# Casting two pairs' queries earlier in the head of a fused retention and MLP kernel

## The chip, the cores and the metric

The kernel runs on one core of one Trainium2 chip. The metric is the device time of one execution in microseconds. The core has a matmul engine (PE, with its weight loads, PEld), a vector engine (DVE), an activation engine (ACT), a general engine (POOL) and a queue engine (SP), each with its own stream of instructions; they wait for each other by semaphores. DMA queues are fed by SP, ACT and POOL.

## The reference

The reference takes queries, keys and values for 8 batches, 8 heads, 576 positions and 64 channels, computes retention (causal scores weighted by a decay per head, with no softmax), and sends the result through a two-layer MLP with a hard-swish:

```python
scores = scale * np.matmul(q, k.transpose(0, 1, 3, 2))
gamma = 1.0 - 2.0 ** (-5.0 - np.arange(H, dtype=np.float32))
Dmat = np.where(rel >= 0, gamma[:, None, None] ** rel[None, :, :], 0.0)   # rel = i - j
ret = scores * Dmat[None, :, :, :]
attn = np.matmul(ret, v)
...
h = x @ w_in                      # 4608 x 512 times 512 x 2048
g = h * np.clip(h + 3.0, 0.0, 6.0) / 6.0
out = g @ w_out                   # 2048 x 512
```

All inputs and the output are float32.

## The kernel before

The 4608 tokens are cut into nine blocks of 512. Block 0, the "heads", holds the first 64 positions of all eight sequences. Blocks 1 to 8 hold positions 64 to 575 of one sequence each, in four chunks of 128. For each block the retention result is brought into a transposed tile `xT`; then come the up product with W_in ("up units", 16 per block, PE into `ph`, ACT makes `u`, DVE makes `g`) and the down product with W_out (`pd`, or in later blocks a Strassen scheme, `pm`).

The order of work on PE, DVE, POOL, ACT and SP is the order in which the program is written (`manual_schedule`); the semaphores are set by a dependency tracker. So a call that stands earlier in the text puts its instructions earlier on each engine that it uses, and an instruction that waits holds up all that follow on its engine.

The change is in the head, lines 738 to 766, where block 0 is prepared. Heads are treated in pairs, 0 to 3. For each pair:

- `load_half` (L403) issues the loads. The queries and pair 0's keys arrive as float32 by the SP and ACT queues, the other keys and the values as float16 by the POOL queue. SP issues one half of the queries of pairs 0 and 1 (ACT the other half) and both halves of pairs 2 and 3, in this order.
- `cast_heads` (L423) turns float32 into float16 on DVE: one instruction for pair 0's keys and one for each pair's queries (tile `hq`).
- `turn_heads` (L428) transposes with eight PE products against the permutation `by_chunk` (tiles `hptk`, `hptq`, in a PSUM pool of two buffers, so the third turn waits for the first's copy) and one copy on ACT or DVE to `hkT` or `hqT`.
- `mask_of_heads` (L123) makes two tiles of decay weights with two exponentials on ACT. Their tile is called `ws` in the profile, since it borrows that tile's memory.
- `scores_heads` (L459) is eight PE products into two PSUM banks (`hpa`) and two DVE products with the masks (L470, tile `ha`).
- `values_heads` (L451) permutes the values by 16 PE products (`hpv`) and copies them on ACT.
- `inner_heads` (L473) is eight PE products (`hpo`) and a copy to `xT`, on ACT or, for pair 2, on DVE.

`idle_products(n)` (L388) issues n pairs of 512-column products of the identity, the two of a pair in two halves of the array, whose result no one reads. Each call takes one buffer from the pool `pp` of six PSUM buffers, which the scores, values and inner products share in rotation.

Behind the head come the first four up units, interleaved over the four pairs' parts of `xT`, with pair 3's inner products in their middle; then units 4 to 15. W_in comes in four pieces of 512 KB on POOL's queue (the first in two halves), then W_out in four. A unit needs the piece of its number divided by four. The loads of chunks 4 to 7 wait on SP until the third issued piece of W_out has landed. While the down product of block 0 runs, POOL scales the queries and values of chunk 4 onward (L207, L210), ACT casts their keys (L203), and PE turns them (`ptk`, `ptq`).

Of the kernel before, what the change touches and what calls it, by code (L numbers as in the profile page):

```python
# [21 lines left out]
def kernel(  # L22
# [100 lines left out]
    def mask_of_heads(i):  # L123

        for h in (2 * i, 2 * i + 1):
            nc.scalar.activation(hmask[:, h, :], dist, ACTF.Exp, bias=scale, scale=float(np.log(gamma[h])))
# [37 lines left out]
    def product(out, lhs, rhs, **flags):  # L164

        for h2 in range(2):
            r = slice(h2 * D, h2 * D + D)
            nc.tensor.matmul(out[r], lhs[:, r], rhs, skip_group_check=True, **flags)  # L168
# [6 lines left out]
    def half_tile(pool, tag, i, dtype, name, **more):  # L175

        if (tag, i // 2) not in pair:
            pair[tag, i // 2] = pool.tile([P, 2, H * D], dtype, tag=tag, name=f"{name}{i // 2}", **more)
        return pair[tag, i // 2][:, i % 2]
# [208 lines left out]
    def idle_products(n):  # L388
        idle = psum.tile([P, NP, P], FP32, tag="pp", name="idle")
        for _ in range(n):  # L390
            product(idle, ident16, ident16.unsqueeze(1).to_broadcast([P, NP, P]), start=True, stop=True)
# [26 lines left out]
    def heads16(i, nm):  # L418
        if nm == "q":
            return half_tile(work, "q16", i, FP16, "hq16_", bufs=2).rearrange("p (e j d) -> p e j d", e=2, j=NJ)  # L420
        return work.tile([P, 2, NJ, D], FP16, tag=f"{nm}16", bufs=dict(k=4, v=NV16)[nm], name=f"h{nm}16_{i}")

    def cast_heads(i, nm, copy):  # L423
        t = heads16(i, nm)
        copy(t, hd[i][nm])  # L425
        hd[i][nm] = t

    def turn_heads(i, nm, copy):  # L428
        pt = psum.tile([P, NJ, P], FP32, tag="st", bufs=2, name=f"hpt{nm}{i}")
        for j in range(NJ):  # L430
            for e in range(2):
                nc.tensor.matmul(pt[e * D:e * D + D, j, :], hd[i][nm][:, e, j, :], by_chunk, start=True, stop=True,  # L432
                                 skip_group_check=True)
        x, y = (NCB, 2 * RP) if nm == "k" else (2 * NCB, RP)
        t = half_tile(work, "qT", i, FP16, "hqT", bufs=3) if nm == "q" else work.tile(
            [P, H * D], FP16, tag="kT", bufs=4, name=f"hkT{i}")
        t = t.rearrange("p (x j y) -> p x j y", x=x, j=NJ)
        copy(t, pt.rearrange("p j (x y) -> p x j y", y=y))  # L438
        hd[i][nm + "T"] = t
# [19 lines left out]
    def scores_heads(i):  # L459
        kT, qT = hd[i]["kT"], hd[i]["qT"]  # L460
        a16 = work.tile([P, 2, NCB, P], FP16, tag="a16", bufs=4, name=f"ha16_{i}")
        pa = [psum.tile([P, NCB, P], FP32, tag="pp", name=f"hpa{h2}_{i}") for h2 in range(2)]
        for c in range(NCB):
            for h2 in range(2):
                r = slice(h2 * D, h2 * D + D)
                nc.tensor.matmul(pa[h2][:, c, :], kT[r, c].rearrange("d j x -> d (j x)"),
                                 qT[r, 2 * c:2 * c + 2].rearrange("d e j r -> d (e j r)"), start=True, stop=True)
        for h2 in range(2):
            m = hmask[:, 2 * i + h2:2 * i + h2 + 1, :].to_broadcast([P, NCB, P])
            nc.vector.tensor_tensor(a16[:, h2], pa[h2], m, ALU.mult)  # L470
        hd[i]["a16"] = a16
# [249 lines left out]
    with tc.manual_schedule(engines={ENG.PE, ENG.DVE, ENG.Pool, ENG.Activation, ENG.SP}):  # L721
        sp, act, pool = nc.sync, nc.scalar, nc.gpsimd
        on_act, on_dve = nc.scalar.copy, nc.vector.tensor_copy
        indices()
        for nm in ("k", "q"):
            landed = load_half(0, nm, 0, sp)
            keys = landed if nm == "k" else keys
            load_half(0, nm, 1, act)
        nc.scalar.activation(warm, half, ACTF.Exp)
        load_half(1, "q", 0, sp)  # L730
        load_half(1, "q", 1, act)
        for i in (2, 3):
            for e in range(2):
                load_half(i, "q", e, sp, keys)
        for i, nm in ((1, "k"), (2, "k"), (3, "k"), (0, "v"), (1, "v"), (2, "v"), (3, "v")):
            for e in range(2):
                load_half(i, nm, e, pool, None if (i, nm) == (1, "k") else keys)
        win_piece(0, 2)
        distances()
        idle_products(5)  # L740
        mask_of_heads(0)
        cast_heads(0, "k", on_dve)
        turn_heads(0, "k", on_act)
        mask_of_heads(1)
        idle_products(3)
        cast_heads(0, "q", on_dve)
        turn_heads(0, "q", on_dve)
        turn_heads(1, "k", on_act)
        mask_of_heads(2)
        idle_products(1)  # L750
        cast_heads(1, "q", on_dve)
        turn_heads(1, "q", on_act)
        mask_of_heads(3)
        scores_heads(0)
        cast_heads(2, "q", on_dve)
        turn_heads(2, "k", on_act)
        scores_heads(1)
        turn_heads(2, "q", on_act)
        turn_heads(3, "k", on_act)
        cast_heads(3, "q", on_dve)  # L760
        scores_heads(2)
        turn_heads(3, "q", on_act)
        values_heads(0)
        scores_heads(3)
        values_heads(1)
        inner_heads(0, on_act)
        values_heads(2)
        inner_heads(1, on_act)
        win_piece(1)
        values_heads(3)  # L770
        inner_heads(2, on_dve)
        first = [up_steps(0, u) for u in range(4)]
        for dmc in range(3):
            for unit in first:
                next(unit)
            if dmc == 1:
                inner_heads(3, on_act)
        for unit in first:
            for _ in unit:
                pass  # L780
        for n in (2, 3):
            win_piece(n)
        wout = [wout_piece(pc) for pc in (0, 2, 1, 3)]
        decays()
        mask_of_chunk()
        others()
        fetch(8, wout[2])
        for u in range(4, NFC):
            up_unit(0, u)
        weight_sums(3)  # L790
        weight_sums(1, 2, 4)
        down = down_plain(0)
        go("k0 D4 k1 D4 +1 k2 D4 +1 k3 D6 h0 D2 c4 h1 D3 h2 D3 h3 D3 D4 c5 t4 D5 a4 s4 u4 D5 z4 t5 c6 D4 "
           "x4 a5 s5 i4 u5 z5 D5 t6 x5 D2 i5 D4 L2 c7 a6 s6 u6 L3 z6 D1 t7 L3 x6 a7 s7 i6 u7 D1 L1 z7 L2 c8 L1 D2 x7 D1 i7 t8 D3 "
           "R3 c9 R3 a8 s8 u8 R2 t9 z8 R4 c10 x8 a9 s9 i8 u9 U1 z9 c11 t10 U3",
           1, down)
        down = down_plain(1)
        go("c12 D6 x9 a10 s10 i9 u10 z10 D2 t11 c13 +1 D7 x10 a11 s11 i10 u11 z11 c14 +2 D8 x11 D2 i11 t12 +1 D3 +1 D3 "
           "a12 s12 u12 t13 D2 c15 D2 z12 +1 D4 x12 a13 s13 i12 u13 z13 D1",
           down=down)  # L800
        go("U1 D3 t14 U1 D2 U1 U1 D2 x13 a14 s14 i13 u14 z14 o1 c16 U1 D2 U1 D2 t15 U1 D2 U1 D2 +1 U1 x14 a15 s15 i14 u15 z15 "
           "c17 D2 U1 D2 +1 U1 D2 +1 U1 D2 x15 +1 U1 i15 t16 c18 +1 U1 D2 t17 U1 U1",
           2, down)
        for kb in range(2, NB):
            for _ in down:
                pass
            plain = kb < FIRST
            down = down_plain(kb) if plain else down_strassen(kb)
            per = 4 if plain else 7
            table = FIRST_STEADY if kb == 2 else STEADY  # L810
            c = NCB * (kb + 2)
            owed = 0
            for u in range(NFC):
                if u == 0:
                    owed += per - 2
                    for _ in range(per - 2):
                        next(down, None)
                if kb + 1 < NB:
                    up_unit(kb + 1, u)
                else:  # L820
                    side_sums(1)
                owed -= per
                while owed < 0:
                    next(down, None)
                    owed += 1
                for w, i in table.get(u, []):
                    if w == "D":
                        for _ in range(i):
                            next(down, None)
                        owed += i  # L830
                    else:
                        do([(w, i if w == "+" else c + i)])
        for _ in down:
            pass
# [30 lines left out]
```

## Time and profile before

The times of three runs are 301.63, 301.76 and 302.48 us, median 301.76. The profiled execution took 302.47 us; its span from the first to the last instruction is 300.7 us.

| What | Value |
|---|---|
| Median of three runs | 301.76 us |
| Profiled execution, its span | 302.47 us, 300.7 us |
| Mean granted PE clock | 0.989 |
| First up product | 18.51 us |
| First product of the keys for block 0's state (`hpk`), behind the last up unit | 33.92 us |
| Last idle time of PE by issue alone | 1.7 us, at 154.25 |

The page of the profile gives for each engine its busy time, its share of the span and its number of instructions, and then the chain that ended last, by engine. A table by stretches gives the busy time of each engine in each stretch, the granted clock (1.00 is full speed), the mean busy share of the DMA engines and their rate. A line of the time order gives the start, the time from the first start to the last end, the engine, the line, the operation, the tiles, the shapes and the count; in brackets is the idle time of the engine ahead of it and what ended it. A line of a DMA issue gives the tile, the queue, the count, the size, and the time from issue to landing.

### The profile page before, as it was taken

Reading aid. Unit: us, or ns where it says so; the run is one execution under the profiler, and the core shown is the slowest. Engines: PE = TensorE matmul, PEld = TensorE weight load, DVE = VectorE, ACT = ScalarE, POOL = GpSimd, SP = SyncE. Lnnn points to the kernel's source line nnn. Section 1 sums busy time; section 2 is a strip of 40 time slices with the busy share of each in tenths; the row PEclk is TensorE's granted clock in tenths of the full one; section 3 lists DMA queues with packets and bytes.
Section 4 is the critical chain, followed back from the end, with each engine's and each line's share of the span. In section 5 each row is a group of like instructions: output and inputs, shape, how many; then the busy total and the mean of one; then the engine's idle time right before and its main releaser. Section 6 shows DMA issues by size and latency. Waiting matters only on the chain.

```text
span 300.7 us, 12600 instructions
## 1 busy us (share of the span) xinstructions
PE 288.2 (96%) x5538; PEld 219.6 (73%) x5538; DVE 213.2 (71%) x387; ACT 196.2 (65%) x361; POOL 135.5 (45%) x176
## 2 busy tenths in 40 slices
PE   5799999899999999999979999999999999999995
PEld 2457666787556667877858878789788977778894
DVE  4728736769895688788875797678768776647554
ACT  4648875899866687586757577657765674565420
POOL 7975068517751912539621962375238003100510
PEclk9969999999999999999999999999999999999999
DMA  6999999996899989998999799789707100200114
GB/s 153 178 196 215 194 251 215 219 224 163 176 205 214 192 193 224 152 220 197 238 236 182 147 258 139 164 182 240 147 4 144 72 2 17 104 25 2 72 72 140
DMA packets 119542, 47.86 MB, mean 159 GB/s; under 512 B 92352, under 2 KB 114880, under 8 KB 119488
## 3 DMA queue, kind: packets, MB, share of 16 engines
q1 hardware_dynamic: 114336, 41.56, 66.7%
q0 software_dynamic: 4720, 5.11, 10.4%
q8 instruction: 43, 0.70, 1.0%
q10 hardware_dynamic: 432, 0.39, 0.4%
q14 instruction: 11, 0.09, 0.1%
HBM read 36.70 MB, written 9.44 MB: 153 GB/s over the span
## 4 chain that ended last, share of the span: by engine, by line
PE 91%; ACT 2%; DMA 2%; DVE 2%; issue 1%; SPq 0%; DVEq 0%; ACTq 0%
PE ph L168 42%; PE pm L168 29%; PE pd L168 9%; PE po L246 4%; PE pa L246 3%; DMA hq<-in_q_dram 2%; PE pu L246 1%; PE ptk L168 1%; PE hptq L432 1%; PE hpo L479 1%; ACT hqT L438 1%; PE hpv L447 1%; PE ptq L168 1%; DVE hq L425 0%; ACT u L510 0%
## 5 line engine op out<-in xcount | busy, mean ns | idle before, releaser
L168 PE MATMUL ph<-xT,win 128*64 128x512 f16 (+1 forms) x1248 | 146.3, 366 | 1.2 <-issue 0.5
L512 DVE SCALAR_TENSOR_TENSOR g<-u,ph 128x512 f16<-128x512 f32 (+1 forms) x156 | 98.6, 643 | 55.1 <-ACT u L510 54.8
L510 ACT ACTIVATE u<-ph,half 128x512 f32<-128x512 f32 (+1 forms) x156 | 100.3, 660 | 44.5 <-PE ph L168 42.5
L168 PEld LDWEIGHTS <-win 128*64 128x64 f16 x1248 | 85.2, 137 | 27.8 <-issue 3.1
L168 PEld LDWEIGHTS <-g 128*64 128x64 f16 x928 | 51.7, 110 | 14.8 <-issue 0.4
L168 PEld LDWEIGHTS <-s 128*64 128x64 f16 x896 | 50.3, 110 | 10.2 <-issue 2.4
L330 POOL TENSOR_TENSOR z<-z,gpow 128x256 f32<-128x256 f32 x24 | 15.8, 659 | 72.2 <-DVE z L329 53.6
L168 PE MATMUL pm<-ws,s 128*64 128x256 f16 x672 | 45.6, 273 | 0.0
L591 POOL TENSOR_TENSOR u<-u,p 128x512 f32<-128x512 f32 x7 | 8.9, 1271 | 62.1 <-ACT u L631 55.8
L382 ACT CAST xT<-po 128x256 f16<-128x256 f32 (+1 forms) x44 | 22.5, 583 | 21.8 <-PE po L246 21.8
L207 POOL TENSOR_TENSOR q<-fq,dec 128x512 f16<-128x512 f32 x32 | 36.7, 1169 | 0.0
L210 POOL TENSOR_TENSOR v<-fv,dec 128x512 f16<-128x512 f32 x32 | 35.1, 1100 | 0.9 <-PE ph L168 0.9
L168 PE MATMUL pd<-wout,g 128*64 128x512 f16 x256 | 34.8, 382 | 0.1
L168 PE MATMUL pm<-wout,g 128*64 128x256 f16 x448 | 31.9, 273 | 0.0
L281 DVE TENSOR_TENSOR a<-pa,mask 128x256 f16<-128x256 f32 (+1 forms) x44 | 21.9, 540 | 7.9 <-PE pa L246 4.7
L203 ACT CAST k<-fk 128x512 f16<-128x512 f32 x32 | 19.9, 622 | 0.0
L527 DVE TENSOR_TENSOR s<-g 128x1024 f16<-128x1024 f16 x28 | 19.2, 689 | 0.2
L336 ACT CAST z<-z 128x512 f16<-128x512 f32 x24 | 14.9, 620 | 5.4 <-DVE z L326 5.0
L168 PE MATMUL pm<-wout,s 128*64 128x256 f16 x224 | 16.5, 273 | 1.8 <-issue 1.7
L168 PE MATMUL pm<-ws,g 128*64 128x256 f16 x224 | 16.6, 274 | 0.0
L527 DVE TENSOR_TENSOR s<-g,s 128x1024 f16<-128x1024 f16 x14 | 12.9, 922 | 0.0
L246 PE MATMUL po<-qT,z 64*64 64x64 f16 x512 | 12.5, 198 | 0.4 <-ACT z L339 0.3
(111 smaller groups left out, 267.5 us busy)
## 6 DMA issues: line engine op xcount, KB each, us to landing
fk<-in_k_dram SPq DMA_DIRECT2D x32, 256.0 KB, 4.5
fq<-in_q_dram SPq DMA_DIRECT2D x16, 512.0 KB, 5.9
fv<-in_v_dram SPq DMA_DIRECT2D x32, 256.0 KB, 5.2
out_dram<-o SPq DMA_DIRECT2D x14, 512.0 KB, 3.1
wout<-in_moe_w_out_dram POOLq DMA_DIRECT2D x4, 512.0 KB, 16.7
out_dram<-o SPq DMA_DIRECT2D x7, 256.0 KB, 5.4
win<-in_moe_w_in_dram POOLq DMA_DIRECT2D x3, 512.0 KB, 10.3
hq<-in_q_dram SPq DMA_DIRECT2D x6, 128.0 KB, 4.9
```

Source lines behind the costliest of these rows:

```text
L168: nc.tensor.matmul(out[r], lhs[:, r], rhs, skip_group_check=True, **flags)
L203: nc.scalar.copy(by_head(k16), in_rows(st[c]["fk"]))
L207: nc.gpsimd.tensor_tensor(by_head(q16[:, e]), in_rows(st[c]["fq"][:, :, e, :]), in_rows(dd[:, NJ + 1 + e, 0:H, :]), ALU.mult)
L210: nc.gpsimd.tensor_tensor(v16, st[c]["fv"], dd[:, NJ, H:2 * H, :], ALU.mult)
L246: return lambda: nc.tensor.matmul(*args, skip_group_check=True, **flags)
L281: nc.vector.tensor_tensor(a16[:, a, 0:n].rearrange("p x i q -> p (x i) q"), pa[a].rearrange("p x i q -> p (x i) q"), m, ALU.mult)
L330: nc.gpsimd.tensor_tensor(new, new, decay, ALU.mult)
L336: nc.scalar.copy(z16, zs[c])
L382: nc.scalar.copy(xt[:, s], po[s].rearrange("p x n (e r) -> p x n e r", e=2))
L510: nc.scalar.activation(uu[:, 0:n], ph[:, 0:n], ACTF.Relu, bias=half, scale=1.0 / 6.0)
L512: nc.vector.scalar_tensor_tensor(out=g[:, hf, ths, jr, :], in0=by_half(uu), scalar=1.0, in1=by_half(ph), op0=ALU.min, op1=ALU.mult)
L527: nc.vector.tensor_tensor(*pend.popleft())
```

## The change

All of the change lies in the order of calls in the head.

- The cast of pair 2's queries comes ahead of pair 0's scores, and that of pair 3's ahead of pair 1's scores. So on DVE each stands ahead of those scores' two mask products.
- Pair 2's queries are turned ahead of pair 1's scores.
- Pair 0's turned queries are copied by ACT and no more by DVE.
- Pair 2's exponentials come ahead of pair 0's query turn, so on ACT directly behind pair 1's; pair 3's come behind pair 0's scores in the text, on ACT again between pair 1's turned queries and pair 2's turned keys.
- The idle products are now 5, 4, 1 and 1 where they were 5, 3 and 1: the four lie ahead of pair 0's query turn, one behind pair 0's scores and one behind pair 1's; the one ahead of pair 1's query turn is gone. That is two more in number; the notes on the change speak of three.

```diff
         mask_of_heads(1)
-        idle_products(3)
+        idle_products(4)
         cast_heads(0, "q", on_dve)
-        turn_heads(0, "q", on_dve)
+        mask_of_heads(2)
+        turn_heads(0, "q", on_act)
         turn_heads(1, "k", on_act)
-        mask_of_heads(2)
-        idle_products(1)
         cast_heads(1, "q", on_dve)
         turn_heads(1, "q", on_act)
+        cast_heads(2, "q", on_dve)
+        scores_heads(0)
         mask_of_heads(3)
-        scores_heads(0)
-        cast_heads(2, "q", on_dve)
+        idle_products(1)
         turn_heads(2, "k", on_act)
+        turn_heads(2, "q", on_act)
+        cast_heads(3, "q", on_dve)
         scores_heads(1)
-        turn_heads(2, "q", on_act)
+        idle_products(1)
         turn_heads(3, "k", on_act)
-        cast_heads(3, "q", on_dve)
         scores_heads(2)
         turn_heads(3, "q", on_act)
         values_heads(0)
```

## The prediction

> **What bounds the kernel now.** I read the page first (busy shares, the slices, the chain), then the first 24 us: busy time by stretches, the waits, PE's order of time, and last the transfers that the first products need.
>
> ```profile
> PE 288.2 (96%) x5538; PEld 219.6 (73%) x5538; DVE 213.2 (71%) x387; ACT 196.2 (65%) x361; POOL 135.5 (45%) x176
> PE 91%; ACT 2%; DMA 2%; DVE 2%; issue 1%; SPq 0%; DVEq 0%; ACTq 0%
> ```
>
> PE carries the chain; other engines have a say almost only in the head. The same in stretches (columns: PE, weight load, DVE, ACT, POOL busy, granted clock, DMA share, GB/s):
>
> ```profile
> 3.94:7.36 3.42, 2.35 (x18) 0.88 (x18) 0.84 (x3) 1.87 (x5) 3.28 (x7) 1.00 1.09 220
> 7.36:10.77 3.41, 3.18 (x44) 2.08 (x46) 1.47 (x3) 2.23 (x6) 2.74 (x6) 1.00 1.30 232
> 10.77:14.18 3.41, 1.90 (x54) 1.39 (x56) 3.30 (x7) 1.77 (x5) 3.40 (x6) 1.00 1.13 137
> 14.18:17.60 3.42, 3.18 (x76) 2.08 (x71) 2.12 (x4) 2.65 (x5) 2.86 (x6) 0.50 1.11 165
> 17.60:21.01 3.41, 3.41 (x38) 1.78 (x38) 0.69 (x1) 1.19 (x3) 2.98 (x17) 0.50 1.24 205
> ```
>
> Between 10.77 and 14.18 PE is busy 1.90 of 3.41 us, and right behind it the granted clock is 0.50 for 6.8 us. (The 1.00 before 10.77 is only the time before the first record: eight query products span 0.64 us at 9.04 and 0.41 at 12.14, so the clock rose at about 10.77.) Where PE stands still in it, from PE's order of time:
>
> ```profile
> 12.14 0.41 PE L432 MATMUL hptq<-by_chunk,hq 128*64 128x128 f16 x8 [1.02 <-DVE hq L425]
> 12.39 0.39 PE L432 MATMUL hptk<-by_chunk,hk 128*64 128x128 f16 x8
> 13.24 0.40 PE L466 MATMUL hpa<-hqT,hkT 64*128 64x128 f16 x8 [0.46 <-ACT hqT L438]
> 13.67 0.41 PE L432 MATMUL hptq<-by_chunk,hq 128*64 128x128 f16 x8
> 14.76 0.61 PE L466 MATMUL hpa<-hqT,hkT 64*128 64x128 f16 x8 [0.24 <-ACT hqT L438]
> 18.51 3.13 PE L168 MATMUL ph<-xT,win 128*64 128x512 f16 x16
> 21.48 0.39 PE L479 MATMUL hpo<-ha,ws 128*64 128x128 f16 x8
> 21.70 12.29 PE L168 MATMUL ph<-xT,win 128*64 128x512 f16 x112
> ```
>
> 1.02 us goes on pair 2's query cast, which stands on DVE behind pair 0's mask products. The x112 are units 0 to 3's second half and 12 units of 0.864 us, so unit 4 begins at 33.92 - 10.37 = 23.5. Two transfers decide what an earlier head is worth: W_in's second piece, issued at 12.55, and the queries of chunk 6, issued at 40.14.
>
> ```profile
> win<-in_moe_w_in_dram POOLq DMA_DIRECT2D x1, 512.0 KB, 8.5
> fq<-in_q_dram SPq DMA_DIRECT2D x1, 512.0 KB, 7.1
> 48.47 2.05 POOL L207 TENSOR_TENSOR q<-fq,dec 128x512 f16<-128x512 f32 x2
> 50.44 0.61 PE L168 MATMUL ptq<-ident,q 128*64 128x128 f16 x16
> ```
>
> **The change part by part.** *Casts on DVE.* Pair 0's turned query leaves DVE for ACT (0.69 us there, 0.59 here); DVE then casts pair 1 when it lands, at 7.5 (second SP issue, 2.4, plus about 5), not at 8.56. Pair 2's queries land by 9.2 (issued at 4.4, rows of 4.8) and are cast at 9.3, ahead of pair 0's mask products; before: 11.53. Pair 3's land at about 10.5 and go behind those two, at 11.1; before: 13.21. What waits behind them on DVE: pair 0's mask products, ready at 9.86, start there at once, since a cast's pitch is 0.48; pair 1's at 11.5 (before 12.01).
>
> *PE's order.* Replayed with the rows' durations (eight products 0.43 us at half clock and 0.22 at full, a copy on ACT every 0.48 and its reader 0.64 behind its start, a mask product every 0.60): query turns at 7.3, 8.6, 10.4, 12.0 (before 7.28, 9.04, 12.14, 13.67); scores at 9.1, 10.9, 11.8, 13.1 (before 9.61, 10.72, 13.24, 14.76). The 1.02 and 0.46 us waits go. The scores of pair 3 come 1.6 us sooner, the last values product at 14.7 instead of 17.54, the last of the three early inner products at 15.4 instead of 18.08.
>
> *Idle products.* Nine become eleven: 3 to 4, and one between pairs 0 and 1, one behind pair 1 for the one taken away. Each is 0.43 us at half clock, 0.21 at full. The fourth fills PE's 0.95 us wait before 7.28: nothing. The other two delay pair 2's key turn by 0.43 and pair 3's by 0.21; both are covered by the wait for W_in below. Uncovered they would cost up to 0.64. They take one more PSUM buffer of the rotation, so pair 2's scores now wait for pair 0's mask products, done at 11.2, before the scores at 11.8: nothing.
>
> *Masks on ACT.* Pair 2's exponentials move ahead of pair 0's turned query, to 6.2 to 6.9, where ACT sat idle until 8.41 (2.15 us): nothing. Pair 3's two (0.69) run at 9.8 to 10.4, before pair 2's keys are ready at 10.7: nothing; if the keys were sooner, at most 0.33 each. No DMA moves: SP's seven issues and POOL's 23 in the head (keys 6, values 8, W_in 5, W_out 4) stand in the same order behind the same waits, so I let their landings stay.
>
> *The clock.* In 7.36 to 10.77 the new order has more products than the 3.18 busy us that raised the clock. In 10.77 to 14.18, counting only the time in which columns stream (0.21 us for eight products at full clock), before has six such groups less a tail, 1.27 us or 37%; the new order nine and a rest, 2.1 us or 61%. The least that kept its clock later in this trace is the stretch with the 1.7 us refill stall near 155, at 45% by the same count. So I take it that the clock stays up; the bound on the other side is that it falls as before.
>
> *What is late next.* Unit 0's products need W_in's first quarter MB: 11.12 + 5.5 = 16.6, so PE waits some 0.8 us there. Unit 4 needs the second piece: 12.55 + 8.5 = 21.05. With the clock up the first four units end at 20.4, and unit 4 starts at 21.1: 2.4 us sooner. With the clock down from 14.18 to 21.01 I get about 22.5: 1.0 sooner. With a drop from 17.6 to 21.0 (PE stood still for W_in, so that is possible): 22.0, or 1.5 sooner. The third and fourth pieces (23.6, 26.1) and the W_out pieces (28.5 to 35.9) land ahead of their use even then.
>
> Behind it stands the load chain of the next chunks. It starts when the third W_out piece lands at 33.5 and is no sooner for a faster PE. Chunk 6's queries land at 40.14 + 7.1 = 47.24. POOL now scales them at 48.47, held by its own work that follows PE; it could start at 47.3 and be done 2.05 later, at 49.35. PE turns the second half of them at 50.44 + 0.22 = 50.66. So at that place no more than 50.66 - 49.35 = 1.3 us survives, whatever the head gained above that. Later loads have more room: chunk 8's queries land some 3 us before POOL takes them.
>
> **Sum.** -2.4 at unit 4, cut to -1.3 at chunk 6. The profiled execution took 302.47 us (span 300.7 and 1.8 around it): 302.47 - 1.3 = 301.2. That execution lies 0.71 above the median 301.76, at the upper end of the runs. Since 1.3 is a floor set by transfers and not a fixed saving, executions of before that are quicker by up to 0.8 (301.63 is the quickest) are nearer to that floor already; I forecast 301.2 for the median too, 0.2% under 301.76.
>
> **Rivals.** *The whole 1.3 counts in the median.* If the spread of the runs (0.85) has nothing to do with the head, each execution loses the same 6.8 us of half clock, and the median falls by 1.3: 301.76 - 1.3 = 300.5. For it: the profile shows the cold stretch following from PE's own waits. Against: the 302.47 and the slowest timed run, 302.48, agree, as if they shared something that the two quick ones lack.
>
> *The cold stretch belongs to some executions alone.* Then the median execution loses hardly any of it and stays at about 301.6 to 301.7. The drop lies on edges 3.41 us apart (10.77, 14.18, 17.60, 21.01); moved against the head by half of that, the busy stretch from 14.8 on would raise the clock 4 to 5 us sooner, and unit 4 would start near 22, within 0.2 of what chunk 6 lets through. [...]
>
> *Slower: PE's refill.* At 154.25 PE stands still for 1.74 us with no releaser but issue, and 0.53 at 199, while the DMA engines are fullest (share 1.46 in 150 to 160). The stream gets eight rows longer and reaches such places at other times against the loads. One more stall of that size gives 301.2 + 1.7 = 302.9; it ends above before once the added stall is over 0.6, and over 1.5 by more than the measurement's bound. For it: the DMA engines are nearly as full elsewhere (share 1.28 in 40 to 45, 1.25 in 90 to 95), without a stall so far. Against: one such stall beside 43 packets of the instruction queue q8. The same mechanism could take the present stall away: 301.2 - 1.7 = 299.5.
>
> **How the numbers follow.** Floor at chunk 6, 301.2 (300.9 to 301.6): 0.38. Whole 1.3 in the median, or the floor with a smaller refill stall, about 300.5 (down to 299.8): 0.36. Refill stall grown, 302.9: 0.17. Cold stretch in few executions, 301.6: 0.09. What a measurement of this kernel can tell from no change is about 0.3%, 0.9 us: 300.85 to 302.67. So faster 0.36, same 0.46, slower 0.18 (a hundredth from the last case's noise). The range reaches down to the second case's middle and a little beyond, 300.1, and up toward the third, 302.5; what it leaves out is most of that third case.
>
> **What would show it.** Right: the query turns' waits of 1.02 and 0.46 gone; granted clock 1.00 in 14.18 to 17.60; a wait of PE for W_in near 16 and near 21; unit 4 at 21.1; chunk 6's queries scaled the moment they land and PE waiting at their turn. Wrong: clock at half in the same stretch; unit 4 at 22.5 or later; no wait at chunk 6 and the lead still over 1.5 us behind it (then the floor isn't one); a refill stall of another size or place; landings of W_in or of chunk 6's queries moved by more than 0.3.

## The result, and the profile after

The changed kernel is slower. Its median is 303.97 us over 20 runs (301.38 to 306.47); the kernel before, beside it on the same chip, has 302.0 over 20 (300.84 to 303.21). The ratio is 1.0064, with a 95% interval of 1.0044 to 1.0083; it leaves out the slowest run, 306.47, which lies over 1.5% above the fastest. The forecast was 301.2. The profiled execution took 305.17 us, with a span of 303.1.

From the page of the changed kernel: PE's row, the row of the queue that brings PE's program, the chain that ended last by engine, and the group of up products (behind the bars: busy time and mean ns, then idle time and what ended most of it).

```profile
PE 287.6 (95%) x5542; PEld 217.1 (72%) x5542; DVE 211.9 (70%) x386; ACT 196.9 (65%) x362; POOL 135.9 (45%) x176
...
q8 instruction: 43, 0.70, 1.0%
...
PE 80%; DMA 10%; POOL 3%; ACT 2%; issue 2%; SPq 1%; DVE 1%; ACTq 0%
...
L168 PE MATMUL ph<-xT,win 128*64 128x512 f16 (+1 forms) x1248 | 147.9, 366 | 5.9 <-issue 3.7
```

PE has four products and four weight loads more: 11,084 of both together, against 11,076. (The recorded expectations count 11,086 and 11,078.) The chain now runs through transfers up to 42.8 us (DMA 10%), 17.4 us of them the wait for the third issued piece of W_out. The last row holds most of the loss: 3.7 us in which the up products waited for "issue", for nothing that the profile names. Before, two groups waited so, for 0.5 and 1.7 us:

```profile
L168 PE MATMUL ph<-xT,win 128*64 128x512 f16 (+1 forms) x1248 | 146.3, 366 | 1.2 <-issue 0.5
...
L168 PE MATMUL pm<-wout,s 128*64 128x256 f16 x224 | 16.5, 273 | 1.8 <-issue 1.7
```

The changed kernel in stretches (columns: PE, weight load, DVE, ACT, POOL busy, granted clock, DMA share, GB/s):

```profile
10.77:14.18 3.41, 3.07 (x94) 2.21 (x94) 3.41 (x7) 2.65 (x6) 3.18 (x6) 1.00 1.07 126
14.18:17.60 3.42, 1.86 (x40) 1.24 (x40) 1.59 (x3) 1.80 (x4) 3.26 (x6) 1.00 1.06 155
17.60:21.01 3.41, 3.12 (x36) 1.90 (x32) 0.17 (x1) 1.48 (x3) 2.94 (x16) 1.00 1.23 205
149.20:152.61 3.41, 3.41 (x145) 2.50 (x142) 2.71 (x5) 1.67 (x3) 0.00 (x0) 1.00 1.19 299
152.61:156.03 3.42, 0.66 (x7) 0.50 (x7) 1.62 (x3) 1.29 (x3) 1.61 (x2) 1.00 1.68 155
156.03:159.44 3.41, 3.41 (x28) 2.93 (x25) 1.29 (x2) 1.19 (x2) 0.00 (x0) 0.50 1.92 196
```

The head runs at full clock, as forecast. But in 152.61 to 156.03 PE is busy for only 0.66 of 3.42 us, and right behind it the clock is at half for 3.41 us. The order of time on PE shows both places:

```profile
9.96 0.41 PE L432 MATMUL hptq<-by_chunk,hq 128*64 128x128 f16 x8 [0.30 <-DVE hq L425]
...
11.55 0.41 PE L432 MATMUL hptq<-by_chunk,hq 128*64 128x128 f16 x8
...
16.79 1.95 PE L168 MATMUL ph<-xT,win 128*64 128x512 f16 x16 [1.10 <-DMA win<-in_moe_w_in_dram]
...
21.10 3.24 PE L168 MATMUL ph<-xT,win 128*64 128x512 f16 x28 [0.38 <-DMA win<-in_moe_w_in_dram]
...
44.08 0.32 PE L246 MATMUL pa<-qT,kT 64*64 64x64 f16 x16 [0.68 <-ACT kT L226]
...
151.19 1.51 PE L168 MATMUL ph<-xT,win 128*64 128x512 f16 x11
155.46 0.93 PE L168 MATMUL ph<-xT,win 128*64 128x512 f16 x5 [2.76 <-issue]
155.95 1.72 PE L168 MATMUL pm<-wout,s 128*64 128x256 f16 x13
```

Laid product against product on the kernel before, the changed kernel leads by 2.33 us at unit 4, by 1.71 behind the wait at 44.08, and by about 1.05 from 50 to 152. Then it stands still for 2.76 us where the kernel before stood for 1.74, and the lead is 0.03; at half clock it loses 1.65 more by 159; a second stand-still, near 200, brings it 2.2 behind, and the last product ends 2.3 later.

### The profile page after: what moved, and what is told of

Same layout as the page of the kernel before. It is cut to its first block, busy times and chain, and to the rows that moved or that the text cites. A ratio compares the mean times of both kernels' runs of the same rounds, so it can differ in the third digit from the quotient of the medians.

```text
span 303.1 us, 12609 instructions
## 1 busy us (share of the span) xinstructions
PE 287.6 (95%) x5542; PEld 217.1 (72%) x5542; DVE 211.9 (70%) x386; ACT 196.9 (65%) x362; POOL 135.9 (45%) x176
## 4 chain that ended last, share of the span: by engine, by line
PE 80%; DMA 10%; POOL 3%; ACT 2%; issue 2%; SPq 1%; DVE 1%; ACTq 0%
PE ph L168 37%; PE pm L168 29%; PE pd L168 6%; DMA wout<-in_moe_w_out_dram 6%; PE po L246 4%; DMA hk<-in_k_dram 3%; PE pa L246 2%; DMA fk<-in_k_dram 2%; POOL win L658 1%; PE pu L246 1%; POOL q L207 1%; PE ptk L168 1%; POOL hv L412 1%; ACT kT L226 0%; ACT u L510 0%
## 5 line engine op out<-in xcount | busy, mean ns | idle before, releaser
L168 PE MATMUL ph<-xT,win 128*64 128x512 f16 (+1 forms) x1248 | 147.9, 366 | 5.9 <-issue 3.7
L168 PEld LDWEIGHTS <-win 128*64 128x64 f16 x1248 | 83.9, 137 | 34.9 <-issue 5.3
L168 PEld LDWEIGHTS <-s 128*64 128x64 f16 x896 | 52.5, 111 | 7.8 <-issue 0.2
L168 PE MATMUL pm<-ws,s 128*64 128x256 f16 x672 | 46.4, 273 | 0.0
L382 ACT CAST xT<-po 128x256 f16<-128x256 f32 (+1 forms) x44 | 22.5, 582 | 22.5 <-PE po L246 22.5
L168 PE MATMUL pm<-wout,s 128*64 128x256 f16 x224 | 18.0, 283 | 0.1
```

The source lines that it names most:

```text
L382: nc.scalar.copy(xt[:, s], po[s].rearrange("p x n (e r) -> p x n e r", e=2))
```

## What PE's stops look like

Both kernels stop in the same two groups of up products, but not at the same product. The kernel before, PE in order of time:

```profile
152.30 1.95 PE L168 MATMUL ph<-xT,win 128*64 128x512 f16 x16
155.99 0.95 PE L168 MATMUL pm<-wout,s 128*64 128x256 f16 x14 [1.74 <-issue]
...
197.80 0.81 PE L168 MATMUL ph<-xT,win 128*64 128x512 f16 x6
199.14 1.30 PE L168 MATMUL ph<-xT,win 128*64 128x512 f16 x10 [0.53 <-issue]
```

(The 0.53 us near 199 come later than the 1.7 that the table of the kernel before calls the last.) The group near 152 is 16 products long. Before, PE gets through all 16 and stops; changed, it stops behind 11. In the group near 197 it stops behind 6 of 16, and changed behind 2. Four products with their weight loads are the eight instructions that the stream got longer. The fifth, near 152, goes with a semaphore instruction: the new order has one more of them on PE in the head (three recorded at L447, before two). Counted in the records of all fourteen profiles of this case, PE stops near 155 behind its 2,908th product in the eight with the old order and behind its 2,907th in the six with the new one, and near 199, wherever it stops there, behind its 3,802nd, whichever products of the work these are. So PE stops at a fixed count of instructions from the start of its program, and not at a fixed place of the work.

The records of q8 fit this: 43 packets of 16,384 bytes, 0.70 MB for some 11,080 instructions, so some 256 in a packet. In all traces here PE's stops lie 256 instructions apart or a multiple of it (recorded instruction 449 + 256 k, where k counts the packets), the packet starts to move at the earliest when PE is near instruction 161 + 256 k, and PE goes on 1.3 to 1.5 us after the packet has come. The two numbers 449 and 161 are a fit of mine, not records. The place near 155 is k = 21, that near 199 k = 28, a third near 230 k = 33. At most other k the time from 161 to 449 is 5.0 us or more in the profiles of the two kernels, longer than the packet needs; at these three, the thin places, it is short for the packet (before: 3.6 us at k = 21, 2.6 at k = 28, 4.7 at k = 33). At the first two, 120 and 128 products of 64 columns lie in it, which PE gets through in 1.4 us. A short time alone made no stop. At k = 35, near 242, it is 3.0 us before and 2.75 changed, and PE does not stop there: the packet starts within 0.4 us of the fitted request, against 3.3 us at k = 21 and 1.1 at k = 28 in the kernel before. In the changed kernel with one-piece idle products (further down) it starts 1.2 us behind the request, and PE's step there is 0.48 us. At the three thin places in the profiles of before and of the change it starts 1.1 to 3.9 us behind. So here the stops went with a packet that started late as well, and what makes it late is not shown here. In idle time the first two stops are 1.74 and 0.53 us before, 2.76 and 0.95 after.

## The experiments

Two theories were weighed. *The count*: the eight instructions shift every later stop against the work, and the thin places get thinner. *The order*: the new order in the head, which leads to other times of loads and packets, costs by itself. All kernels were timed in five rounds beside the kernel before (12 runs each, before 35 in each batch of four).

**Count undone, order kept.** The changed kernel with two idle products less: 11,076 products and loads, as before.

```diff
-        idle_products(5)
+        idle_products(3)
```

> The changed kernel with three idle products at the start in place of five: PE's program has as many rows again as in the kernel before (four fewer loads and four fewer products), all else of the change stays. Theory A (PE's program is refetched in pieces of 256 rows, and eight rows more move two thin places, near 155 and 200, further into want): the time falls to 301.0 to 302.0 us, the stall near 155 is no more than 1.9 us where the changed kernel's profile has 2.8. Theory B (the rows do not matter; PE's lead of 1.0 us from the head meets the loads and transposes of the time near 155 at a worse place): 303 to 304.5 us, stall over 2.3 us. Both: unit 4 starts near 21.1, lead near 1 us in 55 to 150.

301.25 us against 301.5: ratio 0.9998 (0.9973 to 1.0024). The loss is gone. PE's order of time in it:

```profile
150.53 1.94 PE L168 MATMUL ph<-xT,win 128*64 128x512 f16 x15
153.78 0.38 PE L168 MATMUL ph<-xT,win 128*64 128x512 f16 x1 [1.30 <-issue]
...
195.75 1.93 PE L168 MATMUL ph<-xT,win 128*64 128x512 f16 x16
197.51 0.93 PE L168 MATMUL pm<-ws,g 128*64 128x256 f16 x14
```

The stop near 155 is back behind the 15th product and shorter, and the one near 197 has no idle time left to print.

**Count alone, by idle products.** The kernel before with two idle products more: 11,084.

```diff
-        idle_products(5)
+        idle_products(7)
```

> The kernel before with seven idle products at the start in place of five: its PE program is as long as the changed one, its order is the old one. The two more products end inside PE's wait ahead of pair 0's query turn, so the head keeps its time. Theory A: the stalls near 155 and 200 grow as in the changed kernel and no lead pays for them: 303 to 305 us. Theory B: within 0.3% of before, 301.1 to 302.9 us.

303.28 us: ratio 1.0053 (1.0022 to 1.0083). The old order with the new count is slower by about as much as the change. Its profile stops behind 12 of the 16 products near 154 (1.92 us) and behind 2 near 199 (0.53).

**Fewer instructions, the same idle time.** An idle product as one of 128 columns of the array instead of two of 64: the changed kernel has 11,062 products and loads, the kernel before 11,058.

```diff
-            product(idle, ident16, ident16.unsqueeze(1).to_broadcast([P, NP, P]), start=True, stop=True)
+            nc.tensor.matmul(idle, ident16, ident16.unsqueeze(1).to_broadcast([P, NP, P]), start=True, stop=True,
+                             skip_group_check=True)
```

> The changed kernel with every idle product as one product of 128 columns of weights in place of two of 64: the same columns streamed in the same time, but two rows in place of four, so PE's program is 22 rows shorter than the changed one and 14 shorter than before. Theory A: 300.3 to 301.7 us, stall near 155 at most 1.6 us. Theory B: 303 to 304.5 us.

> The kernel before with every idle product as one product of 128 columns of weights: 18 rows shorter, the old order. Theory A: 301.0 to 302.0 us with a stall near 155 of at most 1.7 us, a gain of a few tenths over before. Theory B: no change, 301.5 to 302.5 us.

301.75 us, ratio 1.0016 (0.9986 to 1.0045), and 301.6, ratio 1.0004 (0.9978 to 1.003). All eleven idle products of the change are there, and the loss is not; behind the first five PE waits 0.3 us for pair 0's keys, against 0.2 in the change's profile, so they took about as long. So it is not the idle products' time on PE. Fewer instructions than before bring nothing either: near 155 the stops (1.82 in both) are as long as before's, where at most 1.6 and 1.7 were expected.

**Count alone, without idle products.** The kernel before with four or twelve products of 64 columns behind its three idle products: 11,084 and 11,100 products and loads. The edit for four:

```diff
+        pad = psum.tile([P, NP, P], FP32, tag="pp", name="pad")
+        for _ in range(4):
+            nc.tensor.matmul(pad[0:D, 0, 0:D], ident16[:, 0:D], ident16[:, 0:D], start=True, stop=True,
+                             skip_group_check=True)
```

> The kernel before with eight rows more in PE's program that do next to nothing: four products of 64 by 64 with their weight loads, read by no one, 0.2 us in PE's wait ahead of pair 0's query turn. No idle product of 512 columns is added, so the clock has no reason to change. Theory A (the eight rows move the refills against the program): slower than before by 1.0 to 2.5 us, as with seven idle products at the start. Theory C (it was the two more idle products that cost, by the clock or by PSUM, not their rows): within 0.3% of before.

> The same with 24 rows more (twelve small products, about 0.6 us inside the wait of 0.95). From the trace of before, the time between PE's reaching the place where refill 21 is asked for and the place where it is needed falls from 3.7 to 2.9 us, that of refill 33 from 4.9 to 4.0, that of refill 28 from 2.7 to 2.5. Theory A: slower than before by 1.5 to 4 us, no better than eight rows more. Theory C: within 0.5% of before.

302.46 us, ratio 1.0027 (0.9999 to 1.0055), and 303.16, ratio 1.0038 (1.0007 to 1.0068). Four such products take an estimated 0.1 to 0.2 us of PE, by the idle products' pitch (a pair of 512 columns in 0.21 us at full clock, 0.43 at half); the medians lie 0.8 and 1.5 above before's 301.69, the first below the 1.0 to 2.5 expected. The interval of the first just reaches 1, so alone it does not show a loss. The profile of the second stopped for 1.97 us near 154, behind 4 of the 16 products, twelve products sooner than before, and then the clock fell as in the changed kernel:

```profile
151.92:155.34 3.42, 1.45 (x15) 0.76 (x12) 0.86 (x3) 1.58 (x3) 1.62 (x2) 1.00 1.35 198
155.34:158.75 3.41, 3.41 (x26) 2.15 (x24) 2.82 (x5) 1.86 (x4) 0.00 (x0) 0.50 1.42 227
```

**The same eight instructions elsewhere.** The kernel before with the four small products inside an up unit of a later block, near 256 us (behind all three thin places) and near 167 (behind the first, ahead of the other two; there with (5, 0) for (8, 0)).

```diff
+            for _ in range(4 if (kb, u) == (8, 0) else 0):
+                nc.tensor.matmul(ph[0:D, 0:D], ident16[:, 0:D], ident16[:, 0:D], start=True, stop=True,
+                                 skip_group_check=True)
```

> The kernel before with eight instructions more (four 64x64 products that nobody reads), put near 256 us, behind every place where PE stood still for its program. If it is the place of the packets against the work that counts, nothing ahead of 256 moves: the median stays within 0.15% of before plus 0.1 us for the products (301.4 to 302.2 where before has 301.7), and the stand-still near 155 lies in before's own range, 1.2 to 2.2 us. If the eight instructions cost by themselves, wherever they stand, it is 0.27 to 0.5% above before: 302.5 to 303.2.

> The same eight instructions near 167 us: behind the stand-still near 155, ahead of those near 199 and 230. If the place counts, the one near 155 stays as before (1.2 to 2.2 us), the one near 199 grows from 0.5 to 0.8 or 1.1, and the median is 0.1 to 0.25% above before: 302.0 to 302.5 where before has 301.7. If the loss of the changed kernel and of the eight rows in the head comes from the place near 155 alone, it stays within 0.1%. If it is the rows themselves, 0.27 to 0.5%.

Late: 300.98 us against 301.63 (301.4 to 302.2 expected), ratio 0.9993 (0.9965 to 1.002). Between: 302.42, ratio 1.0025 (0.9998 to 1.0052). Eight instructions cost nothing behind the thin places, though the program is as long as in the two kernels above that lost by eight. Between, the interval still reaches 1. PE's order of time with them late:

```profile
150.46 1.95 PE L168 MATMUL ph<-xT,win 128*64 128x512 f16 x16
153.79 0.96 PE L168 MATMUL pm<-wout,s 128*64 128x256 f16 x14 [1.38 <-issue]
...
195.88 0.81 PE L168 MATMUL ph<-xT,win 128*64 128x512 f16 x6
196.88 1.30 PE L168 MATMUL ph<-xT,win 128*64 128x512 f16 x10 [0.18 <-issue]
```

and between:

```profile
151.02 1.95 PE L168 MATMUL ph<-xT,win 128*64 128x512 f16 x16
153.96 0.95 PE L168 MATMUL pm<-wout,s 128*64 128x256 f16 x14 [1.00 <-issue]
...
196.22 0.38 PE L168 MATMUL ph<-xT,win 128*64 128x512 f16 x2
197.13 1.73 PE L168 MATMUL ph<-xT,win 128*64 128x512 f16 x14 [0.53 <-issue]
```

Late, PE stops behind 16 and behind 6, as in the kernel before; between, behind 16 and behind 2, as before at the first place and as changed at the second. The stop near 199 did not grow from before's 0.53 us, as was expected, so this one profile does not show where the 0.25% went.

**The changed kernel once more.**

> The changed kernel once more, 11086 instructions of PE. If its loss hangs on its number of PE instructions (each 256th packet of the program asked for and used at other places of the work), the stand-still near 155 is again the longest, between 2.3 and 3.6 us, the one near 200 between 0.8 and 1.4, the head's lead at unit 4 about -2.3, and the median stands 0.3 to 0.9% above before: 302.6 to 304.4 where before has 301.7. If the first profile was an odd one (its 2.76 us an accident of one execution), the stand-still near 155 comes out at 1.8 us or less and the span ends below before's 300.7.

302.92 us against 301.63: ratio 1.0045 (1.0016 to 1.0073). The loss is there again. Its profile is a better execution (span 299.7, clock at full throughout from 11.1): the same stops, behind 11 and 2 products, but shorter.

```profile
150.79 1.51 PE L168 MATMUL ph<-xT,win 128*64 128x512 f16 x11
154.12 0.81 PE L168 MATMUL ph<-xT,win 128*64 128x512 f16 x5 [1.81 <-issue]
...
196.53 0.38 PE L168 MATMUL ph<-xT,win 128*64 128x512 f16 x2
197.51 1.73 PE L168 MATMUL ph<-xT,win 128*64 128x512 f16 x14 [0.60 <-issue]
```

The expectations split here. The median lies where the count puts it (302.6 to 304.4 expected). The stop near 155, 1.81 us, lies between the 1.8 or less of an odd first profile and the 2.3 or more of the count, and the span is below before's 300.7, as for an odd profile. So 2.76 us was a high value: the product at which PE stops repeats, the length of the stop does not.

All fourteen profiles together, the step from one recorded start to the next at the three places, in us (so a product's own time is in it):

| Kernel | near 155 | near 199 | near 230 | sum | ratio |
|---|---|---|---|---|---|
| before | 2.12 | 0.91 | 0.18 | 3.21 | 1 |
| changed, count as before | 1.68 | 0.19 | 0.06 | 1.93 | 0.9998 |
| before, 8 late | 1.75 | 0.56 | 0.04 | 2.35 | 0.9993 |
| before, 8 between | 1.38 | 0.91 | 0.45 | 2.74 | 1.0025 |
| before, 8 as small products | 1.55 | 0.91 | 0.48 | 2.94 | 1.0027 |
| before, 8 as idle products | 2.30 | 0.91 | 0.51 | 3.72 | 1.0053 |
| changed, second profile | 2.19 | 0.98 | 0.21 | 3.38 | 1.0045 |
| changed | 3.14 | 1.33 | 0.24 | 4.71 | 1.0064 |
| before, 24 as small products | 2.35 | 0.13 | 0.42 | 2.90 | 1.0038 |
| changed, one-piece idle products | 2.10 | 0.26 | 0.00 | 2.36 | 1.0016 |
| before, one-piece idle products | 2.09 | 0.44 | 0.00 | 2.53 | 1.0004 |
| changed, count as before, loads one piece sooner | 1.40 | 0.30 | 0.06 | 1.76 | 0.9965 |
| before, loads one piece sooner | 1.58 | 0.30 | 0.09 | 1.97 | 0.9974 |
| changed, count as before, loads two pieces sooner | 1.74 | 0.33 | 0.21 | 2.28 | 0.9986 |

Apart from before's own profile, every kernel with a sum of 2.7 or more has a ratio of 1.0025 or more, and every kernel with a smaller sum 1.0016 or less. By place: near 155 the seven profiles with before's count ahead of it have a mean of 1.66, the four with eight instructions more 2.30; near 199 it is 0.43 (six) and 1.01 (five), near 230 0.11 and 0.38. So eight instructions more lengthen the three steps by about 1.5 us together. The four measurements with the eight ahead of all three places (the changed kernel twice) have a mean ratio 0.47% above 1, which is 1.4 us. Single profiles scatter by about as much as the difference, so the table tells direction and rough size; the placing of the stops is exact.

**Loads sooner.** In the head's trace the lead fell at the loads of chunks 4 to 7, which wait for a W_out piece. With the earlier piece as their condition, in the changed order (count as before) and in the kernel before; and with the first piece (`wout[0]`) in the changed order:

```diff
-        fetch(8, wout[2])
+        fetch(8, wout[1])
```

> The changed order with before's number of rows, and the loads of chunks 4 to 7 waiting for the second issued piece of W_out in place of the third, so that they start some 2.4 us sooner. If chunk 6's queries are what swallows the head's lead, the lead of 2.3 to 2.8 us at unit 4 reaches the stretch behind chunk 6 nearly whole: 299.3 to 300.5 us, PE's wait at chunk 6's query turn gone. If they are not, or if the last two pieces of W_out now land too late because they share the DMA engines: 301 to 302 us.

> The kernel before with the same one change of its loads, the control: its PE reaches chunk 6 later than the loads in most executions, so there is little for it to gain; 301.0 to 301.8 us by that reading. If the loads gate the kernel before too: about 300.5 us.

> The changed order with two idle products less (11078 PE instructions, as before) and the load chain of chunks 8 and on started behind W_out's first piece instead of its second. If chunk loads that come late are what swallows the head's lead, it gains again a little on the last version: 300.0 to 300.7 where before has 301.6 (-0.3 to -0.5%). If the loads have all the room they can use, it is the same as with one piece sooner (-0.2 to -0.35%). If loads that start sooner take W_out's later pieces back (those land late and stop the down products), it is at or above before, and PE shows a wait for W_out that was not there.

300.66 us, ratio 0.9965 (0.9938 to 0.9993); 300.99, ratio 0.9974 (0.9949 to 0.9998); and 301.25, ratio 0.9986 (0.9956 to 1.0016). One piece sooner helps either order by about 0.3%, and the first of these is faster than the kernel before. The new order adds 0.09% to it, far less than the intervals tell. Two pieces sooner is no better than one. In the first, the wait at 44.08 is gone, and its lead on the profile of before stays at 2.2 us to 150, though the time falls a little short of the 299.3 to 300.5 expected for that.

## Why the prediction was wrong

**The step that failed** is the costing of the idle products: "the fourth fills PE's 0.95 us wait before 7.28: nothing", and the other two "covered by the wait for W_in". As time in the head that was right (unit 4 starts at 21.33 where each idle product is one instruction pair instead of two, and at 21.10 and 20.99 in the two profiles of the change). But the eight instructions were costed only there, and the sum put their effect on the rest of PE's program at nothing; what they do to the count at 155, 199 and 230 stood only in the rival. With the count undone the loss is gone (0.9998), and with the count alone it comes (1.0053). A step-by-step price was to be had from the profile of before. The stop stood in it behind 16 products, and eight instructions move it four products ahead. At the pitch of 0.105 us in that group PE needs the packet 0.42 us sooner; by the fit it asks for it sooner by only some 0.2, four products of the shorter kind (256 columns, a pitch of 0.05) that lie 288 instructions earlier. So by this estimate each thin place loses about 0.2 us of cover: by three places 0.6 us. The four timed ratios with eight instructions more ahead of 150 (1.0027 to 1.0064) are 0.8 to 1.9 us, so this gives the sign and a third to three quarters of the size. The means of the table put it at 1.5 us. Part of the rest is that packets start later or sooner (2.2 to 3.9 us from the fitted request to the start at the first place), which I can't resolve; in the changed kernel's first profile the half clock behind the stop comes on top.

**The rival that came true** is PE's refill, given 0.17, with 302.9. Its place was right; its price, 1.7 us for one more stall, came as 1.02 more at 155, 0.42 more near 200 and a half clock that was not in it. What spoke against it, "one such stall beside 43 packets", was a poor argument: the places are fixed by the count, and a shift acts on all the places that are thin at once. The prediction also tied the stops to full DMA engines; near 199 they stand at a share of only 0.73 in the kernel before (195 to 200), and PE stops all the same. In the profile the half clock cost 1.65 us, more than the stop's own growth. Of the changed kernel's runs, the nine with a mean granted clock of 0.998 or more have a median of 303.26, the eleven with less 303.99; that the clock fell behind the stop in those eleven is argued from the one profile, not shown.

**The head went as forecast.** The waits of 1.02 and 0.46 us are gone (0.30 is left at 9.96), the query turns stand at 7.06, 8.15, 9.96 and 11.55 (forecast 7.3, 8.6, 10.4, 12.0), PE waits for W_in near 16 and 21, and unit 4 starts at 21.10 (forecast 21.1). The granted clock is 1.00 in 14.18 to 17.60. Some of the agreement is luck: in this profile the clock was up from 5.84 on (eight query products take 0.41 us at 7.06, 0.64 at 7.28 before), where the forecast let it rise at 10.77. In the second profile it rose at 11.14, and unit 4 still starts at 20.99. None of the six profiles with the new order falls to half clock in the head once the clock is up; of the eight with the old order six do, for 3.4 to 10.2 us.

**The cut at chunk 6** was nearly right in size: 1.05 us of lead behind it against 1.3. The places are three, not one: chunk 5's keys at 44.08 (0.68), chunk 6's second half of queries, which POOL had scaled at 49.11 and PE turned at 49.17 (forecast 49.35), and 0.23 for issue at 50. Chunk 5's keys, the first and largest of the three, were not in the prediction: ACT's cast of them had to wait for their landing at 42.8. The queries of chunk 6 landed at 46.95 (issued at 41.75, 5.2 on the way), and what POOL waited for last was PE:

```profile
47.07 2.04 POOL L207 TENSOR_TENSOR q<-fq,dec 128x512 f16<-128x512 f32 x2 [0.26 <-PE po L246]
```

**The second error** is that the 1.3 was carried over to the median. With the old count the new order gives 0.9998 (0.9973 to 1.0024), a gain of 0.8 us at most. Over the profiles here the start of unit 4 in the old order is anywhere from 21.37 to 23.96 (eight profiles, mean 22.5), in the new from 20.60 to 21.44 (six, mean 21.1). The edges of the clock lie elsewhere in each: 10.77 in the profile of before, 13.41 with the eight instructions late, 11.29, 9.41 and 8.73 in others. The late one, in the old order:

```profile
6.58:9.99 3.41, 2.13 (x42) 1.39 (x43) 1.67 (x4) 1.72 (x5) 2.93 (x6) 1.00 1.22 242
9.99:13.41 3.42, 1.60 (x40) 1.19 (x40) 3.42 (x7) 2.11 (x5) 3.17 (x5) 1.00 1.25 153
13.41:16.82 3.41, 3.28 (x76) 2.18 (x74) 2.28 (x4) 2.27 (x5) 3.41 (x7) 0.50 1.04 146
```

Its half clock lasts 3.41 us instead of 6.8, and unit 4 starts at 21.37 without any change to the head. That is the rival of the cold stretch in some executions alone, given 0.09. What sets the place of the edges is not shown. And even where the head is cold, the time hardly shows it: 102 executions of before (the first of each batch left out), ordered by granted clock (below 0.985, to 0.9905, to 0.996, above), have medians of 301.72, 301.51, 301.09 and 301.85 us. So the 6.8 us of half clock in the profile of before were not worth 1.3 in a typical execution. Where the 1.4 us between the two means at unit 4 go by the end, the loads of chunks 5 and 6 tell in part; the rest stays open.

## What to carry to other kernels

An instruction that costs no time where it stands still counts in the engine's program: eight more ahead of PE's stops cost 0.27 to 0.64% here, in four measurements. Before adding or removing some, look for idle time by issue that comes at a fixed count of instructions (here at steps of 256 or a multiple of it), and see how the new count shifts those places against dense runs of short instructions (here 120 and 128 products in 1.4 us); eight instructions added behind the last such place were free here (0.9993). And do not charge a clock stretch seen in one profile to every execution: the 6.8 us of half clock in the profile of before did not show in the medians by granted clock (301.09 to 301.85).

## What the runs showed of the hardware that was not expected

- PE's program comes in packets of some 256 instructions (43 of 16,384 bytes), and PE stood still for 1.0 to 2.8 us near 155 in every profile, always behind the same count of its products (within one). Eight instructions more ahead of such places cost 0.27 to 0.64% (four measurements; the interval of the lowest just reaches 1); the same eight behind all of them cost nothing (0.9993).
- Behind the stop near 155 the clock was at half (0.50) for 3.41 us in the first profile of the changed kernel, where PE had been busy for 0.66 of the 3.42 us ahead (1.65 us lost), and in that of the kernel before with 24 instructions more, where it had been busy for 1.45 of 3.42. In the changed kernel's second profile, at 1.60 of 3.42, the clock stayed up.
